# Attention and a routed expert layer on one core: loads written as steps of the pass, raw weights in quarters, router logits over 256 tokens a matmul, another order of steps

## The chip, the cores and the metric

The kernel runs on one core of a Trainium2 chip. The time is in device microseconds (us) from the start to the end of one execution. Before the change three executions took 663.67, 664.63 and 672.57 us, so the median is 664.63 us.

## The reference

The reference does two things one after the other, in float32.

First comes attention over 8 batches, 8 heads, 576 positions and 64 values a head. Each head's output is the sum of two softmax attentions: one over the sequence averaged in groups of 4 positions (144 of them), repeated back to 576 positions, and one over the full sequence in which a position sees only the neighbours less than 4 away.

```
q_d = q.reshape(B, H, Sd, factor, D).mean(axis=3)      # the same for k and v
out_up = np.repeat(sm_attn(q_d, k_d, v_d), factor, axis=2)
scores = np.where(np.abs(pos[:, None] - pos[None, :]) < 4, scale * q @ k.T, -1e9)
attn_out = out_up + softmax(scores) @ v
```

The result, 4608 tokens of 512 values, goes through an expert layer: `logits = x @ w_gate` over 8 experts, each token goes to the expert with the largest logit, `y = relu(x @ w1[e]) @ w2[e]` with w1[e] of 512 x 1024 and w2[e] of 1024 x 512, and y is scaled by the softmax probability of the chosen expert.

## The kernel before, in words

**Attention runs in passes.** One index is a pair of heads, so there are 32 of them (`NP`). A pass calls a list of small steps, `PASS`, in an order written out by hand: each entry is a step and a lag, and pass i calls the step for pair i minus lag, if there is such a pair. The schedule is manual, so each engine executes its instructions in the order in which the program names them; engines meet only at semaphores. `steps(i)` calls one pass, and after the 32 passes four more (`steps(NP)` to `steps(NP + 3)`) drain the pipeline, with the first expert's work between them.

What one pair goes through, with the lines of the instructions: POOL adds up groups of four columns of q and k (`pool_qk` L207, `pool_qk2` L213) and of v (`pool_v` L218, `pool_v2` L224). TensorE makes the pooled scores (`s_d` L293) and the local ones (`s_loc`: L233 adds the mask, L239 the products). VectorE takes maxima (`max_loc` L252, `max_d` L298), subtracts (`sub_loc` L256), sums (`sums` L262), inverts (L270, L274) and normalises (`norm` L278). ScalarE takes exponentials (`exp_loc` L259, `exp_d` L307), normalises the pooled part (`norm_d` L282) and copies transposed tiles out of PSUM (`e_loc` L324, `e_d` L338); the transposes are TensorE's (`t_loc` L317, `t_d` L330). TensorE multiplies by v (`pv_loc` L345, `pv_d` L358), ScalarE repeats the pooled part (`out_d` L362) and VectorE adds both into `XT` (L373).

**The router** works on blocks of 4 or 5 tiles of 128 tokens, one block every four passes. `r_mm` (L391) multiplies each 128-token tile by the gate weights, padded to 32 columns, so that four tiles lie in four strips of 32 partitions; a fifth tile is put as four partial sums beside them. `r_lg` (L398) copies the logits, `r_turn` (L404, L406) turns them to tokens by experts, and then follow small steps on VectorE and ScalarE (L412 maximum to L449) that find the expert and the gate value. `r_place` (L455 to L459) ranks the tokens, `r_run` L467 and `r_ix` L482 run on POOL. `x_rows` (L508, L510) turns the tokens' values back to rows, and `scatter` (L532, L533) writes 128 rows into the experts' buffer `xs` in DRAM by an indirect DMA from POOL.

**Loads.** All loads of q and k (`load_qk` L117, 583 KB a pair), of v for pooling (`load_vd` L195, 288 KB), of v in windows (`load_vw` L199, 320 KB) and of raw expert weights (L163 to L168, 512 KB each) are issued by SP, in program order. A load waits until the last reader of its buffer is done, and those behind it on SP wait with it. `load_qk(i + 2)`, `load_vd(i + 1)` and `load_vw(i - 1)` stand at the head of pass i, ahead of its steps. The buffers: three for q and k, two for vd, three for vw, five for raw weights. The raw tiles 0 to 4 are loaded whole after passes 10, 14, 18, 22 and 29 (`RAW`), three more after pass 31. The first expert's w1 is split into a high part on ScalarE (`w1_hi`, L182) and a low part on POOL (`w1_lo`, L184), a quarter of a raw tile a pass in passes 15 to 30. `pad_first` (passes 3 and 4) and two more copies (passes 8 and 12) write pad rows into `xs` and `zs`. The table `cst` (523 columns, 261.5 KB) is loaded by ScalarE's queue at the start; its identity matrix is used by every transpose.

**PSUM.** Three banks named pX go round among all transposes and the router, one bank pD holds the pooled scores of one pair (and the inverse sums of the pair before it), and one tile pS the local scores.

**The expert layer** then runs from L657 to L673: for each expert 512 rows are multiplied by w1 and w2, each operand as a high and a low part.

The functions that the change touches:

Of the kernel before, what the change touches and what calls it, by code (L numbers as in the profile page):

```python
# [11 lines left out]
F32 = mybir.dt.float32  # L12
# [32 lines left out]
RAW = (10, 14, 18, 22, 29)  # L45

C_ID, C_TOK, C_CAP, C_DESC, C_LIM = 0, 128, 164, 172, 180
MAXT = 3 + (N - BASE + 127) // 128
C_ALL = C_LIM + E * MAXT
C_SUM = C_ALL + NT + 3  # L50
C_END = C_SUM + 32
# [4 lines left out]
def constants():  # L56
# [23 lines left out]
    c[:, C_SUM:C_SUM + 32] = np.tile(np.eye(32), (4, 1))  # L80
    return c, b
# [7 lines left out]
def attention_moe_kernel(ctx: ExitStack, tc: tile.TileContext, qk, vw, vd, wg, w1, w2, cst, csb, out):  # L89
# [36 lines left out]
    nc.scalar.dma_start(cf, cst)  # L126
# [42 lines left out]

    W1 = {}  # L170
# [26 lines left out]
    def load_vw(i):  # L197
        VW[i] = p2.tile([128, NC, 2, D], F32, name="vw", bufs=3)
        nc.sync.dma_start(VW[i].rearrange("p c h d -> p (c h d)"), vw[i])  # L199
# [184 lines left out]
    def r_mm(m, tiles):  # L384
        T = len(tiles)
        xt = XT[m]
        p = RS[m, "p"] = bank()
        for k, j in [(k, j) for k in range(4) for j in range(4)] + [(k, 4) for k in range(4) if T > 4]:
            c = tiles[j] * 128
            r, o = (j * 32, 0) if j < 4 else (k * 32, 128)  # L390
            nc.tensor.matmul(p[r:r + 32, o:o + 128], wgt[:, k, :], xt[:, k, c:c + 128],  # L391
                             start=(j == 4 or k == 0), stop=(j == 4 or k == 3), tile_position=(0, r),
                             skip_group_check=True)

    def r_lg(m, tiles):
        lg = RS[m, "lg"] = rp.tile([128, 256], F32, name="lg", bufs=1)
        w = 128 if len(tiles) == 4 else 256
        nc.scalar.activation(lg[:, :w], RS[m, "p"][:, :w], AF.Copy)  # L398

    def r_turn(m, tiles):  # L400
        T = len(tiles)
        lg = RS[m, "lg"]
        p = RS[m, "p"] = bank()
        nc.tensor.transpose(p[:, :128], lg[:, :128], ident)  # L404
        if T > 4:
            nc.tensor.matmul(p[:, 128:160], lg[:, 128:], cf[:, C_SUM:C_SUM + 32], start=True, stop=True)  # L406

# [109 lines left out]
    def pad_first(e):  # L517
        r = ROW0 + e * CAP
        nc.sync.dma_start(xs[r:r + FIRST, DM:].rearrange("(t p) c -> p t c", p=128),
                          pad[:, None, DM:].to_broadcast([128, FIRST // 128, ROW - DM]))  # L520
        nc.sync.dma_start(xs[r + FIRST:r + BASE, :], pad)
# [22 lines left out]
    def totals():  # L544
# [3 lines left out]
        over = rp.tile([128, E * MAXT + NT + 3], F32, name="over", bufs=1)  # L548
# [310 lines left out]
    def part(f, n):  # L859
# [4 lines left out]

    PASS = (
        (rc_rk, 6), (rb_turn, 5), (s_d, 1), (eps, 2), (rb_max, 5), (rb_sub, 5), (e_loc0, 3), (rb_top, 5),
        (s_loc, 0), (rb_exp, 5), (pool_qk, -1), (exp_loc, 1), (max_d, 1), (rb_first, 5), (t_d0, 3),
        (rb_gate, 5), (rb_hot, 5), (rb_eps, 5), (inv, 2), (e_d0, 3), (max_scale, 1), (t_d1, 3), (norm, 2),
        (rc_cs, 5), (pool_v2, 1), (e_d1, 3), (rc_last, 5), (x_row, 4), (rc_pos, 6), (max_loc, 0), (inv_d, 2),
        (rc_place, 5), (pv_loc, 3), (rc_run, 6), (pv_d, 3), (sub_loc, 0), (pool_qk2, -1), (rc_ix, 6),  # L870
        (exp_d, 1), (w1_hi, 0), (ra_mm, 4), (out_d, 3), (sums, 1), (t_loc1, 2), (pool_v, 0), (ra_lg, 4),
        (norm_d, 2), (w1_lo, 0), (x_out, 6), (e_loc1, 2), (t_loc0, 2), (add_up, 3),
# [9 lines left out]
    for i in range(NP):  # L882
        if i + 2 < NP:
            load_qk(i + 2)
        if i + 1 < NP:
            load_vd(i + 1)
        if i >= 1:
            load_vw(i - 1)
        if i == NP - 1:
            load_vw(i)  # L890
        if i in (3, 4):
            pad_first(i - 3)
        if i == 8:
            nc.sync.dma_start(xs[0:ROW0, :], pad)
# [5 lines left out]
        if i == 12:  # L900
# [149 lines left out]
```

## Time and profile before

| | us |
|---|---|
| median of three executions | 664.63 |
| the profiled execution | 668.08 |
| its span, first to last instruction | 666.3 |
| TensorE busy | 629.6 |
| VectorE busy | 354.8 |
| ScalarE busy | 342.0 |
| POOL busy | 225.5 |

All times in the rows are microseconds from the first instruction of the profiled execution, unless marked ns. PE is TensorE's matrix multiply, PEld its weight load, DVE VectorE, ACT ScalarE, POOL GpSimd; SPq is SP's queue. Two matmul records stand for each float32 matmul that is not a transpose. L252, the first instruction that VectorE gives to a pair's local scores, is used as the mark of a pass. A granted clock of 1.00 is 2.4 GHz, one of 0.50 is 1.2 GHz.

### The profile page before, as it was taken

What the parts mean: (1) busy time and instruction counts of PE and PEld (TensorE: products, weight loads), DVE (VectorE), ACT (ScalarE), POOL (GpSimd) and SP (SyncE); (2) the same over time, 40 slices, a digit from 0 to 9 for tenths busy, and PEclk for the clock granted to TensorE, in tenths of its full rate; (3) what the DMA queues carried; (4) which work ended last, traced back from release to release, by engine and by line L of the source; (5) the groups of instructions that cost most, each with busy time, mean ns of one, the idle gap of its engine ahead of it and who ended that gap; (6) DMA issues with size and microseconds to landing.
All of it is one profiled execution on the core that took longest, in us unless ns stands there. A gap on an engine that the chain in (4) does not pass through costs nothing.

```text
span 666.3 us, 15915 instructions
## 1 busy us (share of the span) xinstructions
PE 629.6 (94%) x6224; PEld 519.0 (78%) x6227; DVE 354.8 (53%) x691; ACT 342.0 (51%) x941; POOL 225.5 (34%) x348
## 2 busy tenths in 40 slices
PE   7889889999997989999999999999999999999994
PEld 4778777877876978888888888888888888888873
DVE  4969788878875546372274066157127347115020
ACT  2869788988995535362363154345236245224120
POOL 6857779998961610101101110111111101110111
PEclk8979999999997999999999999999999999999998
DMA  8988998897844398284276238328328528110001
GB/s 270 288 221 257 265 286 258 283 272 238 261 140 146 144 262 228 59 229 143 60 179 187 64 104 210 114 88 210 108 63 226 171 92 216 38 46 0 34 17 41
DMA packets 66373, 108.63 MB, mean 163 GB/s; under 512 B 15404, under 2 KB 36668, under 8 KB 66256
## 3 DMA queue, kind: packets, MB, share of 16 engines
q1 hardware_dynamic: 59840, 87.62, 47.1%
q0 software_dynamic: 5984, 19.01, 7.7%
q8 instruction: 67, 1.10, 0.7%
q10 hardware_dynamic: 432, 0.50, 0.3%
q14 instruction: 50, 0.41, 0.2%
HBM read 87.06 MB, written 23.67 MB: 166 GB/s over the span
## 4 chain that ended last, share of the span: by engine, by line
PE 77%; issue 9%; DMA 4%; DVE 4%; ACT 2%; POOL 1%; SPq 0%; another core or an unknown queue 0%; POOLq 0%; ACTq 0%; DVEq 0%
PE p L658 8%; PE p L657 8%; PE p L659 8%; PE p L671 7%; PE p L673 7%; PE p L672 7%; PE pD L293 3%; PE pS L239 3%; PE pPV L345 3%; PE pX L330 3%; PE pPV L358 3%; PE pX L317 3%; PE pX L508 2%; PE pX L772 2%; PE pX L753 2%
## 5 line engine op out<-in xcount | busy, mean ns | idle before, releaser
L678 POOL DMA_INDIRECT out_dram<-y,tix x39 | 37.8, 969 | 213.4 <-ACT y L690 201.7
L657 PE MATMUL p<-xh,w1h 128*128 128x512 f32 (+1 forms) x288 | 106.7, 371 | 1.4 <-ACT xh L604 0.7
L658 PE MATMUL p<-xl,w1h 128*128 128x512 f32 (+1 forms) x288 | 106.1, 368 | 0.8 <-DVE xl L605 0.8
L659 PE MATMUL p<-xh,w1l 128*128 128x512 f32 (+1 forms) x288 | 106.0, 368 | 0.0
L671 PE MATMUL p<-w2h,hh 128*128 128x512 f32 x256 | 101.4, 396 | 0.0
L672 PE MATMUL p<-w2l,hh 128*128 128x512 f32 x256 | 100.1, 391 | 0.5 <-DVE w2l L647 0.5
L673 PE MATMUL p<-w2h,hl 128*128 128x512 f32 x256 | 100.1, 391 | 0.0
L662 DVE SCALAR_TENSOR_TENSOR hl<-p,hh 128x512 fp32r<-128x512 f32 (+1 forms) x72 | 45.5, 632 | 95.9 <-ACT hh L661 94.8
L661 ACT ACTIVATE hh<-p 128x512 fp32r<-128x512 f32 (+1 forms) x72 | 39.6, 550 | 80.5 <-PE p L659 78.3
L690 ACT ACTIVATE y<-p,gi 128x512 f32<-128x512 f32 x32 | 22.0, 688 | 92.2 <-PE p L673 87.8
L657 PEld LDWEIGHTS p<-xh,w1h 128*128 128x128 f32 x288 | 54.4, 189 | 11.8 <-ACT xh L604 1.2
L658 PEld LDWEIGHTS p<-xl,w1h 128*128 128x128 f32 x288 | 54.3, 189 | 10.5 <-DVE xl L605 0.9
L659 PEld LDWEIGHTS p<-xh,w1l 128*128 128x128 f32 x288 | 54.3, 188 | 9.6
L672 PEld LDWEIGHTS p<-w2l,hh 128*128 128x128 f32 x256 | 48.1, 188 | 10.9 <-DVE w2l L647 1.0
L673 PEld LDWEIGHTS p<-w2h,hl 128*128 128x128 f32 x256 | 48.0, 188 | 10.5
L671 PEld LDWEIGHTS p<-w2h,hh 128*128 128x128 f32 x256 | 48.1, 188 | 9.8
L239 PE MATMUL pS<-qk 64*58 64x64 f32 x1280 | 37.2, 223 | 7.7 <-issue 7.1
L647 DVE TENSOR_TENSOR w2l<-raw,w2h 128x512 fp32r<-128x512 f32 x64 | 43.3, 681 | 2.0 <-DMA xs<-xr,ix 1.3
L605 DVE TENSOR_TENSOR xl<-pX,xh 128x512 fp32r<-128x512 f32 x38 | 24.7, 684 | 35.8 <-ACT xh L604 34.8
L533 POOL DMA_INDIRECT xs<-xr,ix x36 | 36.4, 1011 | 16.6 <-DMA gi<-xs 8.2
L182 ACT ACTIVATE w1h<-raw 128x512 fp32r<-128x512 f32 (+1 forms) x72 | 41.8, 580 | 0.0
L646 ACT ACTIVATE w2h<-raw 128x512 fp32r<-128x512 f32 x64 | 39.8, 624 | 2.7 <-DMA xs<-xr,ix 2.7
(150 smaller groups left out, 1276.7 us busy)
## 6 DMA issues: line engine op xcount, KB each, us to landing
raw<-in_w_dram SPq DMA_DIRECT2D x64, 512.0 KB
qk<-in_qk_dram SPq DMA_DIRECT2D x32, 583.0 KB
vw<-in_vw_dram SPq DMA_DIRECT2D x32, 320.0 KB
vd<-in_vd_dram SPq DMA_DIRECT2D x32, 288.0 KB
xrow<-xs SPq DMA_DIRECT2D x32, 192.0 KB
xrow<-xs SPq DMA_DIRECT2D x32, 128.0 KB
xs<-zs SPq DMA_DIRECT2D x6, 512.0 KB
xs<-pad SPq DMA_DIRECT2D x3, 257.0 KB
```

The source lines that it names most:

```text
L182: nc.scalar.activation(hi[:, s], src[:, s], AF.Copy)
L239: nc.tensor.matmul(p[t * 64:t * 64 + QB, s * 512 + c * KW:s * 512 + (c + 1) * KW], x[r, g * QB:(g + 1) * QB], x[r, QPAD + g * QB:QPAD + g ...
L646: nc.scalar.activation(hi, src, AF.Copy)
L647: nc.vector.tensor_sub(lo, src, hi)
L657: nc.tensor.matmul(p, wh[:, fs], xh[:, k, r], start=(k == 0), stop=False)
L658: nc.tensor.matmul(p, wh[:, fs], xl[:, k, r], start=False, stop=False)
L659: nc.tensor.matmul(p, wl[:, fs], xh[:, k, r], start=False, stop=(k == 3))
L661: nc.scalar.activation(hh[:, f, r], p, AF.Relu)
L662: nc.vector.scalar_tensor_tensor(hl[:, f, r], p, 0.0, hh[:, f, r], op0=OP.max, op1=OP.subtract)
L671: nc.tensor.matmul(p, hh, wh, start=(f == 0), stop=False)
L672: nc.tensor.matmul(p, hh, wl, start=False, stop=False)
L673: nc.tensor.matmul(p, hl, wh, start=False, stop=(f == 7))
```

## The change

The pass order `PASS` is replaced by another one. The lags of several steps move: the pooled scores `s_d` from lag 1 to lag 0 (they are made at the end of pass i instead of near the beginning of pass i + 1), `e_loc0` and `t_d1` from 3 to 2, `x_row` from 4 to 5, `rb_eps`, `rc_place`, `rc_cs` and `rc_last` from 5 to 6. The steps of the router stand apart from one another instead of together at the head of the list.

Loads become entries of the list (`ld_qk`, `ld_vd`, `ld_vw`, `ld_x`). `load_vw` has two buffers instead of three. `ld_x` is one small transfer a pass: the pads in halves in passes 3 to 10, and the raw tiles 0 to 4 in quarters of 128 x 256 values in passes 11 to 30.

`r_mm` multiplies 256 tokens at a time: the four row groups of a block of four tiles are two pairs of tiles times two halves of the 512 values, and `r_turn` adds the halves with two matmuls against a table of stacked identities. A fifth tile stays four partial sums. The logits' copy is 128 columns wider. The end of `cst` (from `C_LIM`) is loaded after pass 28 by SP. `over` and `lg` share one buffer.

```
 WARM = (9, 5, 8, 5)
-RAW = (10, 14, 18, 22, 29)
...
-    nc.scalar.dma_start(cf, cst)
+    nc.scalar.dma_start(cf[:, :C_LIM], cst[:, :C_LIM])
...
+    def raw_part(k, j):
+        w, e, i = order[k]
+        if j == 0:
+            raws.append(wpool.tile([128, 1024], F32, name="raw", bufs=5))
+        if w == 1:
+            nc.sync.dma_start(raws[k][:, j * 256:(j + 1) * 256], w1[e, i * 128:(i + 1) * 128, j * 256:(j + 1) * 256])
+        else:
+            r, c = i * 256 + j // 2 * 128, j % 2 * 256
+            nc.sync.dma_start(raws[k][:, j * 256:(j + 1) * 256], w2[e, r:r + 128, c:c + 256])
...
-        VW[i] = p2.tile([128, NC, 2, D], F32, name="vw", bufs=3)
+        VW[i] = p2.tile([128, NC, 2, D], F32, name="vw", bufs=2)
...
         return t
 
     def r_mm(m, tiles):
-        T = len(tiles)
-        xt = XT[m]
+        c = tiles[0] * 128
         p = RS[m, "p"] = bank()
-        for k, j in [(k, j) for k in range(4) for j in range(4)] + [(k, 4) for k in range(4) if T > 4]:
-            c = tiles[j] * 128
-            r, o = (j * 32, 0) if j < 4 else (k * 32, 128)
-            nc.tensor.matmul(p[r:r + 32, o:o + 128], wgt[:, k, :], xt[:, k, c:c + 128],
-                             start=(j == 4 or k == 0), stop=(j == 4 or k == 3), tile_position=(0, r),
-                             skip_group_check=True)
+        for k, a in [(k, a) for k in (0, 2, 1, 3) for a in range(2)]:
+            r = a * 64 + k // 2 * 32
+            nc.tensor.matmul(p[r:r + 32, :256], wgt[:, k, :],
+                             XT[m][:, k, c:c + 512].rearrange("p (u a t) -> p a u t", u=2, a=2)[:, a],
+                             start=(k % 2 == 0), stop=(k % 2 == 1), tile_position=(0, r), skip_group_check=True)
+        for k in range(4) if len(tiles) > 4 else ():
+            r = k * 32
+            nc.tensor.matmul(p[r:r + 32, 256:384], wgt[:, k, :], XT[m][:, k, c + 512:c + 640],
+                             start=True, stop=True, tile_position=(0, r), skip_group_check=True)
 
     def r_lg(m, tiles):
-        lg = RS[m, "lg"] = rp.tile([128, 256], F32, name="lg", bufs=1)
-        w = 128 if len(tiles) == 4 else 256
+        lg = RS[m, "lg"] = rp.tile([128, 384], F32, name="over", bufs=1)
+        w = 256 if len(tiles) == 4 else 384
         nc.scalar.activation(lg[:, :w], RS[m, "p"][:, :w], AF.Copy)
 
     def r_turn(m, tiles):
-        T = len(tiles)
         lg = RS[m, "lg"]
         p = RS[m, "p"] = bank()
-        nc.tensor.transpose(p[:, :128], lg[:, :128], ident)
-        if T > 4:
-            nc.tensor.matmul(p[:, 128:160], lg[:, 128:], cf[:, C_SUM:C_SUM + 32], start=True, stop=True)
+        for u in range(2):
+            nc.tensor.matmul(p[:, u * 64:u * 64 + 64], lg[:, u * 128:u * 128 + 128], cf[:, C_PAIR:C_PAIR + 64],
+                             start=True, stop=True)
+        if len(tiles) > 4:
+            nc.tensor.matmul(p[:, 128:160], lg[:, 256:], cf[:, C_SUM:C_SUM + 32], start=True, stop=True)
 
     def r_max(m, tiles):
         T = len(tiles)
...
     t_loc0, t_loc1, e_loc0, e_loc1 = part(t_loc, 0), part(t_loc, 1), part(e_loc, 0), part(e_loc, 1)
     t_d0, t_d1, e_d0, e_d1 = part(t_d, 0), part(t_d, 1), part(e_d, 0), part(e_d, 1)
 
+    def ld_qk(i):
+        if i >= 2:
+            load_qk(i)
+
+    def ld_vd(i):
+        if i >= 1:
+            load_vd(i)
+
+    def ld_vw(i):
+        load_vw(i)
+
+    def ld_x(i):
+        if 3 <= i < 7:
+            pad_first((i - 3) // 2, (i - 3) % 2)
+        if 7 <= i < 11:
+            h = slice((i - 7) % 2 * 64, (i - 7) % 2 * 64 + 64)
+            nc.sync.dma_start((xs if i < 9 else zs)[h, :], pad[h, :])
+        if 11 <= i < 31:
+            raw_part((i - 11) // 4, (i - 11) % 4)
+
     PASS = (
-        (rc_rk, 6), (rb_turn, 5), (s_d, 1), (eps, 2), (rb_max, 5), (rb_sub, 5), (e_loc0, 3), (rb_top, 5),
-        (s_loc, 0), (rb_exp, 5), (pool_qk, -1), (exp_loc, 1), (max_d, 1), (rb_first, 5), (t_d0, 3),
-        (rb_gate, 5), (rb_hot, 5), (rb_eps, 5), (inv, 2), (e_d0, 3), (max_scale, 1), (t_d1, 3), (norm, 2),
-        (rc_cs, 5), (pool_v2, 1), (e_d1, 3), (rc_last, 5), (x_row, 4), (rc_pos, 6), (max_loc, 0), (inv_d, 2),
-        (rc_place, 5), (pv_loc, 3), (rc_run, 6), (pv_d, 3), (sub_loc, 0), (pool_qk2, -1), (rc_ix, 6),
-        (exp_d, 1), (w1_hi, 0), (ra_mm, 4), (out_d, 3), (sums, 1), (t_loc1, 2), (pool_v, 0), (ra_lg, 4),
-        (norm_d, 2), (w1_lo, 0), (x_out, 6), (e_loc1, 2), (t_loc0, 2), (add_up, 3),
+        (exp_loc, 1), (rb_turn, 5), (t_d0, 3), (rc_place, 6), (eps, 2), (max_d, 1), (inv, 2), (s_loc, 0),
+        (rb_max, 5), (ld_qk, -2), (pool_qk, -1), (w1_hi, 0), (ld_vd, -1), (inv_d, 2), (rb_sub, 5), (ld_x, 0),
+        (pv_loc, 3), (norm, 2), (rb_eps, 6), (e_d1, 3), (rb_top, 5), (rc_rk, 6), (max_scale, 1), (e_d0, 3),
+        (max_loc, 0), (norm_d, 2), (ra_mm, 4), (pv_d, 3), (rb_first, 5), (rc_cs, 6), (rb_exp, 5), (pool_v2, 1),
+        (t_loc1, 2), (rc_last, 6), (rb_gate, 5), (exp_d, 1), (rc_pos, 6), (ra_lg, 4), (out_d, 3), (rb_hot, 5),
+        (pool_qk2, -1), (rc_ix, 6), (t_loc0, 2), (e_loc1, 2), (e_loc0, 2), (ld_vw, 1), (sub_loc, 0),
+        (rc_run, 6), (x_row, 5), (s_d, 0), (x_out, 6), (w1_lo, 0), (pool_v, 0), (sums, 1), (add_up, 3),
+        (t_d1, 2),
     )
 
     def steps(i):
@@ -880,27 +918,13 @@
     load_vd(0)
     steps(-1)
     for i in range(NP):
-        if i + 2 < NP:
-            load_qk(i + 2)
-        if i + 1 < NP:
-            load_vd(i + 1)
-        if i >= 1:
-            load_vw(i - 1)
-        if i == NP - 1:
-            load_vw(i)
-        if i in (3, 4):
-            pad_first(i - 3)
-        if i == 8:
-            nc.sync.dma_start(xs[0:ROW0, :], pad)
         steps(i)
         if i + 1 < len(WARM):
             warm(WARM[i + 1], i >= 3)
         if i == 2:
             nc.vector.tensor_copy(crun, cf[:, C_CAP:C_CAP + E])
-        if i == 12:
-            nc.sync.dma_start(zs, pad)
-        if i in RAW:
-            raw_ahead(RAW.index(i) + 1)
+        if i == 28:
+            nc.sync.dma_start(cf[:, C_LIM:], cst[:, C_LIM:])
         if i == 29:
             early_count()
         if i == NP - 1:
```

## Rows read from the trace of the kernel before

**Rows 1.** Busy time by stretch: us, each engine's busy us (instructions), granted clock, DMA share, GB/s.

```profile
7.75:36.86 29.11, 25.23 (x544) 19.44 (x545) 25.65 (x44) 20.63 (x78) 22.87 (x25) 0.94 0.98 286
36.86:46.50 9.64, 7.13 (x112) 6.17 (x113) 4.80 (x11) 4.30 (x16) 5.67 (x7) 0.65 0.73 197
46.50:93.79 47.29, 42.84 (x1040) 36.66 (x1039) 40.39 (x93) 40.92 (x153) 36.78 (x49) 1.00 0.89 270
...
101.06:185.44 84.38, 78.08 (x1808) 66.14 (x1806) 70.28 (x161) 74.77 (x276) 77.84 (x109) 1.00 0.84 261
...
186.00:216.00 30.00, 25.98 (x471) 20.84 (x469) 17.72 (x43) 21.74 (x76) 10.11 (x16) 0.89 0.45 141
216.00:666.30 450.30, 437.95 (x2035) 360.68 (x2034) 188.31 (x322) 171.48 (x317) 64.19 (x130) 0.99 0.44 123
```

**Rows 2.** Tile mx: count, ns min/median/max, first and last start in us.

```profile
L252 DVE TENSOR_REDUCE mx<-pS x32: 782/817/825, 7.7 to 191.7; 128x10 f32<-128x640 f32 x32
```

**Rows 3.** Timeline of VectorE, 117 to 176: start, us, instruction; those of L252.

```profile
118.14 0.82 DVE L252 TENSOR_REDUCE mx<-pS 128x10 f32<-128x640 f32 x1
...
125.02 0.78 DVE L252 TENSOR_REDUCE mx<-pS 128x10 f32<-128x640 f32 x1
...
141.88 0.82 DVE L252 TENSOR_REDUCE mx<-pS 128x10 f32<-128x640 f32 x1
...
149.97 0.79 DVE L252 TENSOR_REDUCE mx<-pS 128x10 f32<-128x640 f32 x1
```

**Rows 4.** Groups of instructions, 101.06 to 185.44: busy us, mean ns, idle before.

```profile
L533 POOL DMA_INDIRECT xs<-xr,ix x16 | 15.9, 991 | 2.6 <-issue 1.7 <-POOL spacer L532 0.5 <-PE pD L293 0.5
```

**Rows 5.** Waits from 30 to 190: us in total, times, longest us.

```profile
ACT ADT L338 <- PE pX L330: 12.8, 14, 2.2
POOL qkd L213 <- PE pD L293: 10.1, 5, 3.1
...
POOL w1l L184 <- ACT w1h L182: 7.2, 7, 3.2
PE pS L239 <- issue: 7.1, 11, 2.1
...
PE pPV L345 <- issue: 2.6, 1, 2.6
...
DVE rm L412 <- PE pX L406: 1.9, 2, 1.4
DVE rm L412 <- PE pX L404: 1.6, 2, 1.3
```

**Rows 6.** Timelines from 117 to 126 and 141 to 151: the router's instructions.

```profile
119.73 1.30 PE L391 MATMUL pX<-XT,wgt 128*32 128x128 f32 x40
...
121.09 0.38 ACT L398 ACTIVATE lg<-pX 128x256 f32<-128x256 f32 x1
...
146.26 0.28 ACT L398 ACTIVATE lg<-pX 128x128 f32<-128x128 f32 x1 [1.32 <-PE pX L391]
...
147.04 0.19 DVE L412 TENSOR_REDUCE rm<-pX 128x4 f32<-128x32 f32 x1 [1.25 <-PE pX L404]
...
148.78 0.21 DVE L270 RECIPROCAL pD<-smd 128x10 f32<-128x10 f32 x1
```

**Rows 7.** SP's own waits from 0 to 190: us in total, times, longest.

```profile
SPq L195 <- POOL vdt L218: 52.9, 23, 5.3
```

**Rows 8.** The page's DMA queues: packets, MB, share of 16 engines' span.

```profile
q1 hardware_dynamic: 59840, 87.62, 47.1%
...
q8 instruction: 67, 1.10, 0.7%
```

**Rows 9.** Timelines of SP and TensorE in the drain, from 180 on.

```profile
200.14 1.44 SPq L166 DMA_DIRECT2D raw<-in_w_dram  x3
...
211.62 0.81 PE L345 MATMUL pPV<-AT,vw 64*64 64x58 f32 x40 [0.30 <-ACT AT L324]
```

**Rows 10.** Timeline from 34 to 48: the stall of `pv_loc` at 36.8.

```profile
39.37 1.32 PE L345 MATMUL pPV<-AT,vw 64*64 64x58 f32 x35 [2.60 <-issue]
```

More of the change, by code (lines that the diff above doesn't have):

```diff
@@ L44 @@
 WARM = (9, 5, 8, 5)
-RAW = (10, 14, 18, 22, 29)
-C_ID, C_TOK, C_CAP, C_DESC, C_LIM = 0, 128, 164, 172, 180
+C_ID, C_TOK, C_CAP, C_DESC, C_SUM = 0, 128, 164, 172, 180
+C_PAIR = C_SUM + 32
+C_LIM = C_PAIR + 64
 MAXT = 3 + (N - BASE + 127) // 128
 C_ALL = C_LIM + E * MAXT
-C_SUM = C_ALL + NT + 3
-C_END = C_SUM + 32
+C_END = C_ALL + NT + 3
 B_ID, B_TRI, B_MASK = 0, 128, 256
@@ L80, in constants @@
     c[:, C_SUM:C_SUM + 32] = np.tile(np.eye(32), (4, 1))
+    for a in range(2):
+        c[a * 64:a * 64 + 64, C_PAIR + a * 32:C_PAIR + a * 32 + 32] = np.tile(np.eye(32), (2, 1))
     return c, b
@@ L513, in attention_moe_kernel, with pad_first @@
     prev_sc = []
-    def pad_first(e):
+    def pad_first(e, half):
         r = ROW0 + e * CAP
-        nc.sync.dma_start(xs[r:r + FIRST, DM:].rearrange("(t p) c -> p t c", p=128),
-                          pad[:, None, DM:].to_broadcast([128, FIRST // 128, ROW - DM]))
-        nc.sync.dma_start(xs[r + FIRST:r + BASE, :], pad)
+        if half == 0:
+            nc.sync.dma_start(xs[r:r + FIRST, DM:].rearrange("(t p) c -> p t c", p=128),
+                              pad[:, None, DM:].to_broadcast([128, FIRST // 128, ROW - DM]))
+        r += FIRST + half * 64
+        nc.sync.dma_start(xs[r:r + 64, :], pad[half * 64:half * 64 + 64, :])
     def pad_after(e):
@@ L547, in totals @@
         nc.vector.tensor_copy(tot, p[:, :E])
-        over = rp.tile([128, E * MAXT + NT + 3], F32, name="over", bufs=1)
+        over = rp.tile([128, 384], F32, name="over", bufs=1)[:, :E * MAXT + NT + 3]
         nc.vector.tensor_tensor(over[:, :E * MAXT].rearrange("p (e j) -> p e j", j=MAXT),
```

## The prediction

> **What bounds the kernel now.** I read the busy times by stretch first, since the change touches the attention passes and hardly anything behind them. From 216 us on, TensorE is busy 437.95 of 450.30 us, 97%, with the expert layer's matmuls [rows 1]; the reader is to see that two thirds of the time cannot move. The 32 marks of the passes run from 7.7 to 191.7 us [rows 2], 31 intervals of 5.94 us, so all that can be won lies in these 184 us and the drain of about 25 us behind them.
>
> The passes fall into four stretches with different limits [rows 1]. **Early** (7.75 to 36.86, six intervals of 4.85 us): the DMA engines are 98% busy and VectorE 88%; this is a stage of loads. **A stall** (36.86 to 46.50): a single interval of 9.64 us in which every compute engine is idle for a part and the granted clock is 0.65 on the mean, so between the 1.2 and the 2.4 GHz level. **Middle** (46.50 to 93.79, eight intervals of 5.91 us): TensorE 91%, DMA 89%, ScalarE 87%, VectorE 85%. **Late** (101.06 to 185.44, fourteen intervals of 6.03 us): POOL 92%, TensorE 93%, ScalarE 89%, DMA 84%. Here POOL also does the scatters and the low parts of w1.
>
> Then the intervals one by one [rows 3]: 118.14 to 125.02 is 6.88 us and 141.88 to 149.97 is 8.09 us, and the three between them take 16.86 us, 5.62 each. The two long ones hold a block of the router. So late passes without a router run at 5.62, and a router costs (6.88 + 8.09) / 2 - 5.62 = 1.87 us, once in four passes. POOL sets the floor of the late stretch: 77.84 us busy, and 2.2 us more of its own gaps ahead of scatters (1.7 issue, 0.5 spacer [rows 4]) make 80.04 of 84.38. So at most 4.3 us can be won there, whatever the order does, because POOL's instructions stay as they are.
>
> The waits [rows 5] tell which engines block each other: ScalarE behind the transposes of the pooled part 12.8 us, POOL behind `s_d` 10.1, POOL behind ScalarE's high part of w1 7.2, VectorE's first router step behind the turned logits 1.9 and 1.6. TensorE is idle ahead of `s_loc` for 7.1 us with no releaser that the profile shows. Most of the first two cost nothing late, where POOL is full in total.
>
> **The change, part by part.**
>
> *Order of the router's steps.* Today ScalarE waits 1.32 us for the router's matmul, then VectorE waits 1.25 us for the turned logits, and from L412 at 147.04 to the inversion at 148.78 VectorE goes through the router's small steps with only `max_d` between them, waiting for ScalarE's exponential [rows 6]. The new list puts `ra_mm` eleven entries ahead of `ra_lg` with `pv_d` and `t_loc1` between, and `max_d`, `inv` and `s_loc` between the turn and the maximum; the later steps have `norm` and `max_loc` between them. So VectorE's own work covers the answers of the others, and the 1.25 us goes. Late there are 3.5 blocks in 14 passes: 3.5 x 1.87 = 6.5 us of delay, of which POOL's floor leaves 4.3; I take 3.0 (0 to 4.3). What is late next there is POOL. Middle: two blocks in eight passes, 2 x 1.25 = 2.5 us.
>
> *Router matmul.* 40 records of 128 columns take 1.30 us [rows 6], 0.0325 each. After it they are 16 of 256 columns and 8 of 128: by records 0.78 us, by columns (5,120 both times) 1.30. The four strips still take turns, which is why I exclude a loss. Taken by records, since 128 columns at 0.0325 us already run overlapped: 0.52 us a block. Late POOL covers it; middle 2 x 0.5 = 1.0 (0 to 1.0). The wider logits' copy adds 0.38 - 0.28 = 0.10 us on ScalarE [rows 6] seven times, 0.7 in all, hidden as ScalarE is 87 to 89% busy; without that cover it costs 0.7. One more matmul in the turn is nothing beside it.
>
> *Loads as steps.* SP executes its own queue, so where a load stands in the pass matters only by what stands ahead of it on SP and by what its buffer waits for. The order on SP stays q/k, vd, vw; vd still waits for `pool_v` of two pairs before, today 52.9 us in 23 waits [rows 7]. Only vw changes: with two buffers it waits for `pv_loc` of the same pass. It then has almost two passes until its use, about 11 us at 5.94 a pass. I count nothing; if a load came late, POOL or `pv_loc` would show a DMA as its releaser. SP's added issues, one a pass at 1.44 / 3 = 0.48 us [rows 9], fall into its waiting.
>
> *Raw quarters and pads.* By the code the five raw tiles go from 768 packets to 2,560, 1,792 more, over 20 passes and 16 engines: 5.6 an engine and pass. A mean packet of the hardware queue takes 47.1% x 666.3 x 16 / 59,840 = 84 ns [rows 8], so at most about 0.47 us a pass if a small packet cost as much as a mean one, and 0 if it costs by bytes. Late, 16% of 6.03, that is 0.96 us a pass, are free on the DMA engines [rows 1]. I take 0.
>
> *Table loaded later.* 247 of 523 columns, 126 KB by the code, leave the head; at the early 286 GB/s [rows 1] 0.4 us. VectorE is 88% busy beside, so I take 0.2 (0 to 0.4).
>
> *`s_d` at the end of the pass.* It moves by some eight entries across the pass's boundary; its bank still waits for `exp_d` and `norm`. POOL's 10.1 us of waits for it lie mainly in the stall stretch, where POOL has time. I count 0. `x_row`, `rc` and the rest change place, not number: 0.
>
> *Drain.* vw of the last pair is now issued in `steps(NP)`, behind the first expert's rows and three raw tiles (issued 200.14 to 201.58). 1.57 + 0.33 MB at the middle's 270 GB/s land 7.0 us later, about 208.6, and `pv_loc` needs it at 211.62 [rows 1, 9]: 0. At the drain's mean of 141 GB/s it would be 13.5 us, 215.1, a loss of 3.5.
>
> *The stall.* At 36.76 TensorE stops inside `pv_loc` for 2.60 us with no releaser shown [rows 10], the clock falls, and the interval is 9.64 instead of 4.85, 4.8 us lost [rows 1]. The page's instruction queue moved 67 packets of 16 KB [rows 8], and such an idle within a row of equal matmuls, whose operands lie in the same tiles as those before it, looks like instructions that come late while the DMA engines are 98% busy. Neither is changed: 0 (-4.8 if it goes).
>
> The Trainium skill, in "Runtime: NRT & Kernel Launch", section Instruction fetch mechanics, says that engines refill in 16 KiB blocks and that crossing one is mostly hidden. By that rule the stall would have a cause that the order could remove, and the sum would be 4.8 us lower; the 2.60 us row disagrees with "hidden", as far as it goes.
>
> **Sum**, against the profiled execution of 668.08 us: 0.2 + 3.0 + 2.5 + 1.0 = 6.7, so 661.4. That execution is 3.45 us above the median of 664.63; with the same distance the median after is 657.9, so **658 us**.
>
> **Rivals.** (a) *Nothing shows.* What the router gives back is taken by TensorE and POOL, both over 90% busy in the late stretch, and the idles without a releaser stay. For it: TensorE 93% late; against: 1.87 us a block. 662 to 667, median 664. (b) *Everything goes*: the stall 4.8, late 4.3, TensorE's idle in the middle 47.29 - 42.84 = 4.45 and 1.0 of the matmul, head 0.4: 15 us, 650. For it speaks that no engine is full in the middle; against it that the idles ahead of `s_loc` have no releaser that the order would touch. (c) *Slower: the quarters fill the DMA engines*, in passes 11 to 30. It decides from 0.96 us / 5.6 = 171 ns an added packet, twice the mean of 84; at 250 ns it is (1.40 - 0.96) x 20 = 8.8 us, so 673. Against: 84 ns is a mean over larger packets.
>
> The Trainium skill's "DMA: Bandwidth & Descriptors", section Bandwidth, wants transfers of 1 MiB and more, which speaks for (c) and against 128 KB quarters; no row of the kernel before has a 1 KB packet's time by itself.
>
> (d) *The change does less than it says*: SP ignores places in the list; that is in my sum already.
>
> **Chances.** Forecast 0.50 (654 to 662), (a) 0.27, (b) 0.14, (c) 0.05, and 0.04 for a late vw or another stall like the one above (668 to 671). The range is 648 to 668: it leaves out (c), half of the last case and a little of (b). Over 2%, about what a measurement of this kernel can tell from no change, is 13.3 us: below 651.3 lie most of (b) and little of the forecast, 0.13; above 677.9 a worse (c), 0.03; between them 0.84.
>
> **What would show it.** In the changed profile late intervals of about 5.8 us with POOL at 95% and none above 7; L412 no longer behind L404 and L406; 24 records of L391 in about 0.8 us; no DMA as releaser of `pv_loc`; DMA share below 0.95 in passes 11 to 30. I am wrong if router passes stay at 7 us, if SP waits for vw's buffer hold up q and k, or if TensorE's idle without a releaser grows.

## The result and the profile after

The changed kernel takes 657.71 us (median of four executions, 655.53 to 659.64) where the kernel before took 664.65 beside it: a ratio of 0.9864, 95% interval 0.9815 to 0.9913. Run again later on another chip it gave 655.21 against 663.56, 0.9876 (0.9832 to 0.9920). So the change makes the kernel 1.3% faster, inside the 2% that were called no change and by about what the forecast's sum said. The parts of the sum did not come out as they were priced, and most of what follows is about that. Ratios leave out executions that were disturbed (of order_only, below, eight of eleven), so one can differ from the quotient of two medians.

The profiled execution took 659.64 us (span 657.9), 8.4 less than that of before. Busy time by stretch of the changed kernel, with the columns of [rows 1]:

```profile
7.50:36.70 29.20, 26.13 (x548) 19.25 (x549) 25.09 (x45) 21.76 (x80) 21.45 (x23) 0.94 1.00 256
36.70:48.50 11.80, 10.33 (x256) 8.06 (x252) 9.85 (x21) 9.73 (x36) 8.08 (x9) 1.00 0.94 278
...
95.90:176.40 80.50, 77.12 (x1766) 63.33 (x1768) 69.61 (x165) 75.41 (x282) 75.18 (x106) 1.00 0.93 280
176.40:206.00 29.60, 26.77 (x424) 21.52 (x418) 17.95 (x40) 21.14 (x70) 12.13 (x18) 0.83 0.52 164
206.00:657.90 451.90, 440.05 (x2057) 362.36 (x2057) 188.75 (x324) 172.10 (x319) 65.48 (x130) 1.00 0.43 123
```

The stretches are cut at the same marks as before, and the early one is as long as it was (29.20 us for six intervals). The stall is gone as such: two intervals take 11.80 us at the full clock, where one took 9.64 at 0.65. In the late stretch, fourteen intervals again, 5.75 us each instead of 6.03, the DMA share rose from 0.84 to 0.93, and TensorE is now the fullest engine (77.12 of 80.50, 96%) with ScalarE (94%) and POOL (93%) behind it. The marks themselves (L264 is the old L252):

```profile
L264 DVE TENSOR_REDUCE mx<-pS x32: 814/817/826, 7.5 to 181.5; 128x10 f32<-128x640 f32 x32
```

The 31 intervals span 174.0 us, 10.0 less than in [rows 2]; behind the last mark the changed kernel loses 1.8 us (657.9 - 181.5 = 476.4 against 474.6).

The marks around router blocks, from VectorE's timeline of the changed kernel:

```profile
112.67 0.82 DVE L264 TENSOR_REDUCE mx<-pS 128x10 f32<-128x640 f32 x1
118.94 0.81 DVE L264 TENSOR_REDUCE mx<-pS 128x10 f32<-128x640 f32 x1
...
134.82 0.82 DVE L264 TENSOR_REDUCE mx<-pS 128x10 f32<-128x640 f32 x1
142.05 0.81 DVE L264 TENSOR_REDUCE mx<-pS 128x10 f32<-128x640 f32 x1
```

These are 6.27 and 7.23 us, so a router pass is still longer than its neighbours, as in [rows 3]. The timeline of all engines, 110 to 120, shows that the order around the router did what it should, and that the matmul did not:

```profile
112.74 1.07 PE L401 MATMUL pX<-XT,wgt 128*32 128x256 f32 x16
...
113.63 0.40 PE L406 MATMUL pX<-XT,wgt 128*32 128x128 f32 x8
114.44 0.55 ACT L412 ACTIVATE over<-pX 128x384 f32<-128x384 f32 x1
...
116.94 0.57 PE L418 MATMUL pX<-cf,over 128*128 128x64 f32 x4
...
117.45 0.22 DVE L282 RECIPROCAL pD<-smd 128x10 f32<-128x10 f32 x1
117.75 0.20 DVE L427 TENSOR_REDUCE rm<-pX 128x5 f32<-128x40 f32 x1
```

VectorE takes the maximum (L427) without waiting: the 1.25 us of [rows 6] are gone. The matmul runs from 112.74 to 114.03, 1.29 us for 24 records, against 1.30 us for 40.

Waits from 30 to 190 in the changed kernel (us in total, times, longest):

```profile
POOL qkt L219 <- DMA qk<-in_qk_dram: 8.2, 6, 1.8
DVE mxd L310 <- PE pD L305: 7.5, 11, 1.3
...
PE pPV L357 <- issue: 4.7, 8, 1.5
...
PE pS L251 <- issue: 2.8, 5, 1.5
...
ACT ADT L350 <- PE pX L342: 1.9, 5, 1.2
```

ScalarE's wait for the pooled transposes fell from 12.8 to 1.9 us, POOL's for `s_d` and for w1's high part are gone from the list's head [rows 5]. VectorE now waits for the pooled scores (7.5). A POOL wait for q and k (8.2) is the only one with a DMA behind it; `pv_loc` has none. TensorE's idle with no releaser ahead of `s_loc` fell from 7.1 to 2.8, that ahead of `pv_loc` rose from 2.6 to 4.7; the one that answers to [rows 10] is this, from TensorE's timeline, 36 to 39:

```profile
38.21 0.73 PE L357 MATMUL pPV<-AT,vw 64*64 64x58 f32 x34 [1.47 <-issue]
```

SP's own waits from 0 to 190 and two of the page's DMA queues, to be put beside [rows 7] and [rows 8]:

```profile
SPq L207 <- POOL vdt L230: 79.3, 29, 5.0
SPq L211 <- PE pPV L357: 27.5, 12, 4.9
...
SPq L119 <- PE pS L251: 2.5, 1, 2.5
```

```profile
q1 hardware_dynamic: 62080, 87.78, 48.0%
...
q8 instruction: 66, 1.08, 0.7%
```

SP's waits changed places: it stands for vd's buffer 79.3 us and for vw's 27.5, and at the loads of q and k (L119) for 2.5 only. In the kernel before the same view has these beside the 52.9 us of [rows 7]:

```profile
SPq L117 <- PE pX L330: 39.7, 16, 5.2
SPq L117 <- PE pS L239: 16.9, 7, 3.7
...
SPq L117 <- PE pX L508: 7.8, 2, 6.0
```

That is 64.4 us at the loads of q and k, on which vd and vw, behind them in the queue, waited as well. The queue has 2,240 packets more (the forecast had 1,792 for the raw quarters), and its share rose from 47.1 to 48.0%.

### The profile page after: what moved, and what is told of

It is laid out like the page before. It is cut to its first block, busy times and chain, and to the rows that moved or that the text cites. A ratio compares the mean times of both kernels' runs of the same rounds, so it can differ in the third digit from the quotient of the medians.

```text
span 657.9 us, 15721 instructions
## 1 busy us (share of the span) xinstructions
PE 629.9 (96%) x6123; PEld 513.0 (78%) x6123; DVE 352.3 (54%) x691; ACT 343.7 (52%) x941; POOL 226.5 (34%) x348
## 3 DMA queue, kind: packets, MB, share of 16 engines
q8 instruction: 66, 1.08, 0.7%
## 4 chain that ended last, share of the span: by engine, by line
PE 80%; issue 8%; DMA 3%; DVE 3%; ACT 2%; POOL 1%; another core or an unknown queue 0%; POOLq 0%; SPq 0%; DVEq 0%; ACTq 0%
PE p L675 8%; PE p L674 8%; PE p L676 8%; PE p L690 7%; PE p L688 7%; PE p L689 7%; PE pD L305 4%; PE pX L342 3%; PE pPV L357 3%; PE pPV L370 3%; PE pX L329 3%; PE pS L251 3%; PE pX L523 2%; PE pX L789 2%; PE pX L770 2%
## 5 line engine op out<-in xcount | busy, mean ns | idle before, releaser
L675 PEld LDWEIGHTS p<-xl,w1h 128*128 128x128 f32 x288 | 54.9, 191 | 10.4 <-DVE xl L622 0.9
L219 POOL TENSOR_TENSOR qkt<-qk 128x576 f32<-128x576 f32 x32 | 36.7, 1146 | 15.7 <-DMA qk<-in_qk_dram 15.7
```

Of the source, the lines that this page charges most:

```text
L675: nc.tensor.matmul(p, wh[:, fs], xl[:, k, r], start=False, stop=False)
```

## The experiments

Every kernel is read by its ratio to the kernel before on the same chip, since chips differ (the kernel before had medians of 663.87, 658.17 and 663.56 us in the three series). Beside the ratio I use two numbers from each profile. The first is the sum of TensorE's idles over 0.3 us between the first and last mark that end with no releaser: the profile shows nothing that TensorE waited for, and calls the wait "issue". The second is TensorE's whole idle in the stretch 55 to 150, the same 95 us of every kernel.

| kernel | us | ratio, 95% | marks' span | idles "issue" | idle 55-150 |
|---|---|---|---|---|---|
| before | 664.65 | 1 | 183.9 | 11.1 | 7.97 |
| order_only | 668.88 | 0.9991 [0.9929, 1.0053] | 184.6 | 15.5 | 8.75 |
| router_only | 665.95 | 1.0048 [1.0020, 1.0077] | 180.8 | 10.4 | 5.98 |
| loads_only | 660.48 | 0.9957 [0.9921, 0.9993] | 176.7 | 7.8 | 4.96 |
| order_router | 660.56 | 0.9959 [0.9925, 0.9994] | 178.5 | 13.3 | 7.02 |
| or_rest | 658.85 | 0.9933 [0.9889, 0.9977] | 178.7 | 10.6 | 6.02 |
| or_vw | 656.12 | 0.9895 [0.9848, 0.9942] | 169.4 | 5.8 | 2.39 |
| after_whole | 650.30 | 0.9880 [0.9829, 0.9930] | 166.4 | 1.5 | 1.50 |
| changed | 657.71 | 0.9864 [0.9815, 0.9913] | 173.9 | 7.2 | 3.73 |
| changed, again | 655.21 | 0.9876 [0.9832, 0.9920] | 171.0 | 3.8 | 3.79 |
| after_oldrouter | 665.19 | 1.0007 [0.9973, 1.0040] | 182.1 | 12.9 | 8.06 |
| before_lite | 656.33 | 0.9969 [0.9933, 1.0005] | 173.8 | 6.5 | 1.16 |
| order_lite | 656.91 | 0.9981 [0.9940, 1.0022] | 172.5 | 8.0 | 2.11 |
| after_lite | 650.53 | 0.9873 [0.9814, 0.9933] | 168.3 | 0.4 | 1.31 |

One profiled execution stands behind each number of the last three columns, and the two of the changed kernel (7.2 and 3.8) show how much such a number scatters.

The sum holds two kinds of idle. Number all of TensorE's records (matmuls, weight loads and its sequencer's own) in order of start: in the fourteen profiles each of the 39 idles over 1 us ends at a number that leaves 190 to 194 when it is divided by 256, whatever the instruction. So they stand at borders between blocks of 256 instructions; I call the idles there stops. The idles at other numbers I call pauses. In the kernel before and the changed one they are about 0.4 us each and make 4.1 of the 11.1 us and 2.1 of the 7.2; before, most stand in the rows of `s_loc`. Their cause was not tried.

**One part at a time.** Only the new list, with everything else as before:

```
-        (rc_rk, 6), (rb_turn, 5), (s_d, 1), (eps, 2), ...
+        (exp_loc, 1), (rb_turn, 5), (t_d0, 3), (rc_place, 6), ...     # the changed list without ld_*
```

> The kernel before with the new list of steps alone (loads at the head of the pass, raw tiles whole, three vw buffers, old router matmul). Theory 'order': the list gives the whole gain, about 7 us, so 657 to 660 us and pass marks that span 174 to 176 us instead of 184. Rival 'loads': the gain comes from the smaller, evenly spread transfers, which spare TensorE the idles without a releaser; then 663 to 666 us here. Rival 'router matmul': also 663 to 666 us here.

Measured 0.9991, with a median of 668.88 against 663.87 us: no gain that shows, where the forecast had 5.5 of its 6.7 us in the list. The wait it should take away went (no wait of L412 for the turned logits stands in its list of waits), but TensorE's idles without a releaser grew from 11.1 to 15.5 us, the most of any kernel.

Only the router's matmul, copy and turn, under the old list:

```
-        for k, j in [(k, j) for k in range(4) for j in range(4)] + ...:     # 128 tokens a matmul
+        for k, a in [(k, a) for k in (0, 2, 1, 3) for a in range(2)]:       # 256 tokens a matmul
```

> The kernel before with the new router matmul, copy and turn alone. Theory 'order' and rival 'loads': no change, 663.5 to 665.5 us, since 16 records of 256 columns take 1.07 us in the changed kernel, as long by columns as before. Rival 'router matmul': 660 us or less.

Measured 1.0048, 3 us slower, where I had counted 1.0 us as a gain. Under the old list VectorE still waits for the turn (L418 <- L412 2.6 us and <- L409 1.4), which is now four matmul records and two more instead of three. But that is 4.0 us where the kernel before has 3.5 [rows 5], so it doesn't make the 3 us; where the rest lies stays open.

Only the loads (steps at the head of the old list, quarters, halves, the table in two parts, three buffers for vw):

```
+        (ld_qk, -2), (ld_vd, -1), (ld_vw, 1), (ld_x, 0),
         (rc_rk, 6), (rb_turn, 5), (s_d, 1), (eps, 2), ...
```

> The kernel before, old list of steps and old router, with raw tiles in quarters, pads in halves, the table's end loaded late, and the loads as the first entries of the list (three vw buffers). Theory 'order': 663.5 to 665.5 us. Rival 'loads': 657 to 660 us, and the interval of 9.64 us at 36.86 is gone. If small transfers cost more than their bytes: above 666 us.

Measured 0.9957, so what I had put at 0.2 us gives about 3. The stall is not gone in it: one interval still takes 8.4 us, from 29.91.

The new list and the new router together, with the old loads:

> New list of steps and new router, old loads. Theory 'order': 657 to 660 us, equal to the order alone within 1 us. Rival 'loads': 663 to 666 us. If only the list and the router together give the gain (the list was made for the new router), this one is 3 us or more below the order alone.

Measured 0.9959. The three ratios of the single parts make a product of 0.9996; by their intervals an estimate of 0.992 to 1.007. The changed kernel has 0.9864. This comparison lacks one part, since loads_only keeps vw's old place and its three buffers. That the parts don't add is shown by the router: alone it costs 0.5%, and in the changed kernel, as the last run below shows, it is worth 1.3%.

**The quarters.** The changed kernel with raw tiles loaded whole, in passes 11, 15, 19, 23 and 27:

```
-        if 11 <= i < 31:
-            raw_part((i - 11) // 4, (i - 11) % 4)
...
+        if i in RAW:
+            raw_ahead(RAW.index(i) + 1)
```

> The changed kernel with raw tiles 0 to 4 loaded whole again, in passes 11, 15, 19, 23 and 27; all else as changed. Theory 'late instructions': TensorE's idles without a releaser come from its instruction packets queueing behind bursts of loads; whole tiles bring them back, from 7.9 us in the changed profile to 11 to 14, and the median to 660 to 663 us, as with the new list and new router under the old loads (660.56). Rival 'other loads': the vw buffers, halved pads or the late table gave the gain of the loads; then 657 to 658.5 us and idles of about 8 us.

Measured 0.9880, the changed kernel's ratio; so the quarters neither cost nor give anything that shows beside intervals of half a percent, and the theory that small transfers let instructions come in time fell on this run: it asked for idles of 11 us or more, and they are 1.5, the fewest of any kernel that does all the work.

**Fewer loads.** To see what the loads cost each order, three kernels leave out the loads of q and k of pairs 12 to 29 and compute with the tile of three pairs before instead:

```
     def load_qk(i):
+        if 12 <= i < 30:
+            QK[i] = QK[i - 3]
+            return
```

> The kernel before without the q and k loads of pairs 12 to 29, which take the tile of three pairs before; about 1.0 instead of 1.6 MB a pass is moved from pass 10 to 28. Theory 'late instructions': TensorE's releaserless idles between marks 12 and 30 fall below 2 us, from about 7, and the mean interval there from 6.05 to 5.6 to 5.7 us, where POOL's 5.6 to 5.75 holds it. Rival 'the idles belong to the order': idles and 6.05 us stay.

> The new list alone, without the same q and k loads. Theory 'late instructions': the list by itself is the better one and only drew more idles (15.5 us in its profile); with the traffic gone its interval between marks 12 and 30 falls from 6.46 to 5.5 us, 0.1 to 0.2 below the old list without these loads, and equal to the changed kernel without them within 0.1. Rival 'the list alone is worse': 6.0 us or more.

> The changed kernel without the q and k loads of pairs 12 to 29. Theory 'late instructions': interval between marks 12 and 30 from 5.77 to about 5.5 us, TensorE over 95% busy, releaserless idles below 2 us there. Rival 'TensorE and POOL alone set it': 5.7 us as with the loads.

The ratios hide the effect, because at the end, when the loads come back for pair 30, these kernels stand still (10.26 and 7.11 us for two intervals in before_lite). The stretch 55 to 150 shows it. Columns as in [rows 1], first the kernel before, then before_lite, then after_whole, then after_lite:

```profile
55.00:150.00 95.00, 87.03 (x2044) 74.07 (x2041) 78.95 (x182) 83.03 (x308) 80.88 (x111) 1.00 0.89 275
```

```profile
55.00:150.00 95.00, 93.84 (x2307) 81.09 (x2298) 88.09 (x201) 92.72 (x350) 88.16 (x122) 1.00 0.61 186
```

```profile
55.00:150.00 95.00, 93.50 (x2249) 77.15 (x2248) 84.75 (x198) 92.12 (x343) 90.28 (x125) 1.00 0.94 293
```

```profile
55.00:150.00 95.00, 93.69 (x2261) 77.16 (x2253) 85.56 (x198) 92.23 (x349) 90.11 (x125) 1.00 0.62 188
```

With the old list, dropping a third of the traffic (DMA share 0.89 to 0.61) takes TensorE's idle from 7.97 to 1.16 us and puts 263 more matmuls into the same 95 us; with the new list and old router the idle goes from 8.75 to 2.11. In after_whole there is hardly anything left to win by it: 1.50 with all loads at a DMA share of 0.94, against 1.31 in after_lite. The changed kernel itself, 3.73 and 3.79 in its two profiles, lies between. So most of the old kernel's idle in this stretch came from its loads, which my prediction held to be off the path, and the changed kernel carries the same bytes at a higher rate and loses about half as much. Of the 7.97 us, 6.0 are idles without a releaser, of which 0.9 are left in before_lite.

One expectation fell. order_lite was to run 0.1 to 0.2 us a pass faster than before_lite; from mark 12 to 29, ahead of the standstill, it takes 5.61 us a pass and before_lite 5.36, with after_lite at 5.47 (with all loads: 6.08 before, 5.79 changed). So in these single profiles the new list is no faster in itself. What it gives, it gives beside the loads.

**Which loads.** Between order_router (0.9959) and after_whole (0.9880) lie vw's place and buffers, and the small loads' times. Each alone, on top of order_router, beside the changed kernel again:

```
-        VW[i] = p2.tile([128, NC, 2, D], F32, name="vw", bufs=3)
+        VW[i] = p2.tile([128, NC, 2, D], F32, name="vw", bufs=2)
...
-        if i >= 1:
-            load_vw(i - 1)
...
+        ... (e_loc0, 2), (load_vw, 1), (sub_loc, 0), ...
```

> The new list and the new router with the old loads, which alone gave 0.996, and in addition vw as in the changed kernel: two buffers, issued late in the pass behind the matmul that frees it. Theory 'vw' (the place of that load is the missing 0.8%, since it no longer comes in one burst with q, k and vd): ratio 0.988, mean interval from mark 12 to mark 30 below 5.75 us. Theory 'small loads' (pads in halves, table late, raw tiles in passes 11 to 27): 0.996, intervals 5.9 us. Theory 'late instructions' (what differs is how much TensorE waits without a releaser, which depends on where the instruction blocks fall and not on any one load): anything from 0.985 to 1.0, and the span of the marks follows the sum of those idles, 11 us in the kernel before, 7 in the changed one.

```
-RAW = (10, 14, 18, 22, 29)
+RAW = (11, 15, 19, 23, 27)
...
+        if 3 <= i < 7:
+            pad_first((i - 3) // 2, (i - 3) % 2)
+        if 7 <= i < 11:
...
+        if i == 28:
+            nc.sync.dma_start(cf[:, C_LIM:], cst[:, C_LIM:])
```

> The new list and the new router with q, k, vd and vw as in the kernel before, but pads in halves in passes 3 to 10, the table's end late, whole raw tiles in passes 11, 15, 19, 23 and 27. Theory 'vw': 0.996, intervals from mark 12 to mark 30 of 5.9 us. Theory 'small loads': 0.988, and the gain lies in the first twelve intervals, where the pads are, since the marks 12 to 30 see of it only the raw tiles. Theory 'late instructions': anything from 0.985 to 1.0, in step with TensorE's idles without a releaser.

> The changed kernel itself, beside the next three on the same chip. All theories: ratio to the kernel before 0.986 (0.981 to 0.991), as before. If the ratio came out above 0.993, the difference between this kernel and the one with only the list and the router's matmul (0.996) would be no more than the scatter between chips.

Measured 0.9895 for vw and 0.9933 for the small loads. The intervals overlap, so the ratios lean to vw and don't decide. The profile's stretch is clearer, with one profile each. The rows are those of order_router, or_rest and or_vw:

```profile
55.00:150.00 95.00, 87.98 (x1988) 72.41 (x1992) 77.88 (x180) 84.19 (x311) 81.05 (x113) 0.98 0.85 266
```

```profile
55.00:150.00 95.00, 88.98 (x1956) 72.68 (x1950) 77.48 (x180) 84.52 (x307) 81.24 (x113) 0.98 0.85 262
```

```profile
55.00:150.00 95.00, 92.61 (x2162) 76.07 (x2160) 84.11 (x195) 91.46 (x339) 89.67 (x122) 1.00 0.94 296
```

TensorE idles 2.39 us in or_vw, against 7.02 in order_router and 6.02 in or_rest. It is tempting to say that the late vw takes a burst of loads apart, but SP's timelines of order_router and or_vw don't show it:

```profile
112.44 0.32 SPq L198 DMA_DIRECT2D vd<-in_vd_dram  x1
112.81 0.34 SPq L202 DMA_DIRECT2D vw<-in_vw_dram  x1
113.24 0.38 SPq L120 DMA_DIRECT2D qk<-in_qk_dram  x1
```

```profile
113.35 0.32 SPq L198 DMA_DIRECT2D vd<-in_vd_dram  x1
114.22 0.33 SPq L202 DMA_DIRECT2D vw<-in_vw_dram  x1
114.60 0.42 SPq L120 DMA_DIRECT2D qk<-in_qk_dram  x1
```

From 55 to 150 vw starts 0.4 us (median) behind vd in order_router and 0.6 in or_vw, and the next q and k 1.1 and 0.4 us behind vw: the three loads stand as close together with vw late as with vw early. Why vw's place helps stays open.

**The old router under the new list and loads.** Since router_only had lost 3 us, the changed kernel with the old router might have been the best of all:

```
-            nc.tensor.matmul(p[r:r + 32, :256], wgt[:, k, :], ...
+            nc.tensor.matmul(p[r:r + 32, o:o + 128], wgt[:, k, :], xt[:, k, c:c + 128], ...
```

> The changed kernel with the router's matmul and turn of the kernel before (128 tokens a matmul, one transpose); the rest as changed. By the run of the router alone, 1.005, the new matmul costs 3 us (VectorE and ScalarE wait for the longer turn and copy): then 0.982, 3 us faster than the changed kernel beside it, and the better version. Rival: under the new list the turn and the copy are covered, and the two matmuls take the same time by columns: 0.986, no difference. A third way: the new list needs the two row groups of the new form, so that this one is slower than the changed kernel: 0.99.

Measured 1.0007, beside 0.9876 for the changed kernel on the same chip: of the three ways the last had the direction, and none the size. A term that I had put at 1.0 us, and that alone costs 3, is worth 1.3% here, the whole gain. Its profiled execution (669.91 us, 4.7 above its median) shows a way in which that happens. TensorE's timeline, 134 to 176, two router passes:

```profile
135.74 1.08 PE L403 MATMUL pX<-XT,wgt 128*32 128x128 f32 x32
141.54 1.65 PE L520 MATMUL pX<-cf,XT 128*128 128x128 f32 x7 [3.26 <-issue]
...
164.54 1.28 PE L403 MATMUL pX<-XT,wgt 128*32 128x128 f32 x34
168.71 0.42 PE L403 MATMUL pX<-XT,wgt 128*32 128x128 f32 x6 [2.90 <-issue]
```

The second idle falls between the 34th and the 35th of 40 equal matmuls that read the same tiles: no operand can be late there. DMA packets by queue around the first, which lasts from 138.28 to 141.54; first 136 to 139.2, then 139.2 to 140.3:

```profile
q1 hardware_dynamic: 240, 0.72, 76.6%
q0 software_dynamic: 79, 0.26, 20.3%
```

```profile
q1 hardware_dynamic: 148, 0.30, 101.9%
q8 instruction: 1, 0.02, 6.0%
```

The packet of 16 KB with TensorE's next instructions begins only after TensorE has stopped, is on its way for 1.05 us among full DMA engines, and TensorE goes on 1.25 us after its end. What such an idle costs is more than itself:

```profile
135.40:148.80 13.40, 9.35 (x158) 7.34 (x152) 5.23 (x13) 7.08 (x24) 11.39 (x17) 0.75 0.75 237
```

The interval is 13.4 us at a granted clock of 0.75. In all three profiles with the new list and the old router (order_only, order_lite and this one) an idle over 1 us stands inside the router's matmul (2.1, 1.2 and 2.9 us), in two of them another within the transposes of `x_rows` (1.4 and 3.3); in the seven with the new list and the new router none stands at either place. By the numbering above, the stop inside the matmul has the same place in all three (numbers 6847, 6847 and 6850), with six of the 40 records left: the count of instructions ahead decides what stands at a border, and the new router has fewer of them.

## Why the prediction was right, and where its steps failed

The total came out within 0.3 us of the forecast, on the likeliest case's mechanism only in part, so that closeness is luck. Interval by interval, the profiled executions differ so (before minus after; marks counted from 0):

| stretch | forecast | measured |
|---|---|---|
| marks 0 to 6 | 0.2 at the head | 0.2 at the head, 29.11 - 29.20 = -0.1 behind it |
| marks 6 to 7, the stall | 0 | 9.64 - 6.22 = 3.4 |
| marks 7 to 15, middle | 2.5 + 1.0 | 47.29 - 44.72 = 2.6 |
| marks 15 to 16 | none | 7.27 - 8.21 = -0.9 |
| marks 16 to 30, late | 3.0 | 84.38 - 80.50 = 3.9 |
| marks 30 to 31 | none | 6.26 - 5.09 = 1.2 |
| behind the last mark | 0 | -1.8 |

**The router's order, late and middle.** The sizes fit, the mechanism does not hold by itself. In the middle, marks 7 to 15, TensorE's stops fell from 3.6 to 1.0 us, as much as the whole gain there; that the waits for the turned logits had been priced at 2.5 is a coincidence. Late, 2.3 of the 3.9 us lie in the three router passes (22.45 to 20.19 us; the forecast counted 3.5 of them) and the rest in the other eleven; there the pauses fell from 4.1 to 1.7 us and the stops from 0.8 to 0.4. The 1.87 us a router was itself priced from an interval of 8.09 us that holds a stop of 0.80. From TensorE's timeline, first the two largest stops of the middle and the one inside the router's matmul in the kernel before, then two stops of the changed kernel:

```profile
74.95 0.55 PE L239 MATMUL pS<-qk 64*58 64x64 f32 x22 [1.48 <-issue]
...
93.32 0.43 PE L239 MATMUL pS<-qk 64*58 64x64 f32 x11 [2.10 <-issue]
...
145.78 0.42 PE L391 MATMUL pX<-XT,wgt 128*32 128x128 f32 x6 [0.80 <-issue]
```

```profile
54.97 0.68 PE L357 MATMUL pPV<-AT,vw 64*64 64x58 f32 x30 [0.58 <-issue]
...
88.32 0.57 PE L357 MATMUL pPV<-AT,vw 64*64 64x58 f32 x22 [0.79 <-issue]
```

The waits went as said, yet the list alone gives 0.9991. The step that failed is "so VectorE's own work covers the answers of the others, and the 1.25 us goes": it went, and TensorE's idles without a releaser took its place (15.5 us). This is what the prediction had named as a sign of being wrong; in the changed kernel it did not grow, in order_only it did. Its bound was wrong too. I took POOL for the late floor, at 80.04 us; or_vw and after_whole go below it (79.71 and 79.12), and TensorE is now the fullest engine (96% late, and 93.50 of 95 in after_whole). POOL is 93% busy late, not 95%, and router passes are still 6.3 to 8.2 us.

**The router's matmul.** Priced by records, 0.52 us a block; by columns, nothing, and the rows say columns: 379 ns (median) for a record of 256 against 273 for one of 128, four strips at a time, 1.29 us a block against 1.30. The prediction had both ends in its range and took the wrong one. Under the old list the router alone costs 3 us, and under the new list and loads it gives 1.3%; neither was in any term.

**Loads as steps and vw.** "I count nothing" is the second step that failed. The added waits for vw's buffer (27.5 us) are indeed harmless, no DMA releases `pv_loc`, and POOL's wait for q and k is small in both (4.9 us before, 8.2 after). But I argued from the instructions that wait for the data, which were few, and not from what else comes over the same DMA engines: TensorE's instructions do, and before_lite shows what the loads cost TensorE.

**The stall.** It was left at 0 with "Neither is changed", and -4.8 as the other end, and 3.4 us of it went. The Trainium skill, in "Runtime: NRT & Kernel Launch", section Instruction fetch mechanics, has the fetch of a 16 KiB block mostly hidden. In the trace most blocks are, and the others are dear: between the marks of the changed kernel there are 29 such packets for 7,452 matmuls and weight loads, about 257 each, and two of them have a stop of over 1 us behind them; in the kernel before it is 3 of 30, in order_only 8 of 30. In all profiles here the idles over 1 us without a releaser (up to 3.4 us) end 1.2 to 1.8 us behind the end of such a packet. These stops are the term that I had mis-sized most, and it is a term of several stretches, not of one stall: between the marks they make 7.0 us in the kernel before, 13.1 in order_only, 5.2 and 0.9 in the changed kernel's two profiles. Over the eleven profiles that do all the work, the marks' span rises by 1.3 us for each us of stops and pauses together (correlation 0.92), and the kernels' ratios go with them too (0.75).

**What is shown and what is argued.** Shown: TensorE's long idles stand at borders between blocks of instructions, behind a packet of the instruction queue; with fewer loads the old order loses most of its idle from 55 to 150; raw tiles whole or in quarters give the same within half a percent; list and loads without the new router give nothing. Just clear of the noise is vw's place (0.9895 against 0.9959); a gain from the small loads (0.9933) is not shown. Argued: that the packets come late because they wait behind the loads. For it speaks how late a packet starts, counted from the moment at which TensorE begins the block ahead of the one that the packet brings: from 55 to 150 at most 5.0 us in the kernel before and 3.2 in before_lite, 4.7 and 3.0 in order_only and order_lite, 3.4 and 2.7 in the changed kernel and after_lite. Lateness alone is not enough, since after_whole has one of 4.5 us and only 0.4 us of idle behind it. And no run could change the fetch alone, and the kernels with fewer loads also get their data earlier. Why the old router form loses so much under the new list stays open. It puts 40 matmuls and 40 weight loads into 1.3 us where the new one has 24 of each, which uses up instructions faster just before the transposes, but that is a reading of three profiles. A rival was not tried: that the form matters only by moving the borders. Some dozens of added instructions ahead of the passes would move them and change little else.

**Quarters, pads, drain.** Rival (c) is out: after_whole and the changed kernel agree, so small packets cost nothing that can be measured here, though the DMA share rose to 0.93 late. In the drain the cover held: vw of the last pair is issued at 192.08 behind three raw tiles, and its `pv_loc` at 202.99 shows no wait for it. The 1.8 us lost behind the last mark are between the last passes, where the clock was 0.83 instead of 0.89: at the 1.2 GHz level for 10.2 us (192.6 to 202.8) where the kernel before has 6.8. It is not vw's new place: after_whole has that too, and loses 0.2.

## What to carry to other kernels

Where the DMA engines are 85 to 95% busy, ask of every load what else its packets may delay, and read TensorE's idles that have no releaser as a resource of their own: sum them over the stretch, look whether they end shortly after a packet of the instruction queue, and whether the instructions that end them lie a multiple of one number apart. Where a load can stand at two points of a pass at equal cost, measure both: here the issue times did not tell which was better. And parts of one change that touch the same resource don't add: the router's new form costs 0.5% alone and gives 1.3% in company, so an edit that loses alone isn't yet a bad edit.

## What was not expected of the hardware

- TensorE stops for 1.0 to 3.4 us at a border between blocks of 256 instructions, often in the middle of equal matmuls, with a 16 KB packet of the instruction queue (0.9 to 1.4 us) close by, and resumes 1.2 to 1.8 us after the packet's end. Stops make 0.4 to 13.1 us of a kernel.
- With float32 in four strips of 32, a matmul of 256 columns takes 379 ns where one of 128 takes 273, and the row of them as long as by columns (1.07 us for 16 against 1.08 us for 32).
- The length of an idle does not tell by itself what becomes of the clock. In after_oldrouter the clock was at the 1.2 GHz level from 140.0 to 146.8, from within the idle of 3.26 us on; after its idle of 2.90 us, 165.82 to 168.71, it stayed at 2.4 GHz up to 204.8. In the changed kernel an idle of 1.53 us, up to 30.38, was followed by 3.4 us at 1.2 GHz (32.2 to 35.6), and one of 1.47 us by none.
